# Seven buffers instead of four between two matrix layers, with a smaller GpSimd DMA scratch

## The chip, the core and the metric

The kernel runs on one core of one Trainium2 chip. The metric is the device time of one execution in microseconds (us), as the median of several runs; lower is better. TensorE (PE) multiplies, VectorE (DVE), ScalarE (ACT) and GpSimd (POOL) work on elements, and SyncE (SP) issues nearly all DMAs.

## The reference

Block-causal attention feeds one wide layer pair, which feeds a second one with a three-way maximum:

```python
scores = where(block_i >= block_j, q @ k.T / 8, -1e9)       # 4 batches, 8 heads, 576 tokens, dim 64
x = (softmax(scores) @ v).reshape(2304, 512)
h = maximum(x @ w_in, 0)                                    # 512 -> 2048
x = (s * (h * h) + b) @ w_out                               # 2048 -> 512
h = maximum(maximum(x @ w1, x @ w2), x @ w3)                # 512 -> 768
out = h @ w_out2                                            # 768 -> 512
```

## The kernel before, in words

**Precision.** TensorE reads a reduced 32-bit format, so each operand is kept as two halves, a high part and the remainder, and a product is three matmuls (high by high, high by low, low by high). Making the halves is a copy on ACT or DVE and a subtraction on DVE (`sub_to`, L364). The weights arrive as 64-bit floats; `convert` loads a tile of 128x512 (L679) and rebuilds 32-bit floats with a clamp (L683), a rescaling on ACT or POOL, and three bit operations (L691, L695, L700) on DVE.

**Stages.** First comes attention, 16 head pairs in turn; the result lies in `xf`, 128 partitions by 4 slabs by 2304 tokens, and `normalize` (L791) divides by the softmax sums, which come back through DRAM (`scr`, L785). Then comes the first layer pair, on five chunks of tokens (512, 512, 512, 384, 384). Its inner dimension of 2048 is 16 tiles `f_` of 128, and the kernel takes the first 8 (`HF = 8`) for all chunks and then the last 8. The second layer pair follows and isn't touched.

**The stretch that the change concerns.** While attention ends, not all weights are prepared. So for chunks 0 and 1 all of the first layer runs first: `l1(c, f_)` for `f_` 0 to 7 and both chunks, 16 tiles of 12 matmuls, each followed by four ACT steps and one subtraction on DVE, which leave a tile of 128x1024 (both halves) in a buffer of the strip `h1`. Only then the second layer `l2(c, f_, k)` runs, again 12 matmuls for each chunk and `f_`, adding into all eight PSUM banks. `h1` has four buffers (`HAT1`, four places of 1024 words in the big SBUF tile `arena`), so the tiles of `f_` 0 to 5 go out to DRAM (`hscr`, L952, "away"), and those of 6 and 7 stay. The second layer therefore starts with 6 and 7 (`late_`), and `l1_back` (L961) fetches the other twelve tiles, each into the buffer that a tile just used has left:

```python
late_ = [HF - 2, HF - 1] + list(range(HF - 2))
...
        if i + 2 < HF:
            for c in range(2):
                l1_back(c, late_[i + 2])
```

**Places in `arena`.** `places` lays out the strips one after another: 8 tiles of `w_in`, 4 of `x1`, 8 of `w_out`, then `h1`; `RN` is the end. The attention operands (`kq_at`) lie at the end of the same tile, counted back from `RN`. The split input of chunk 1 (`x1b`, written by `split_x(1, "x1b")`) borrows four of the `w_out` places.

**Order.** `Sched` records each operation with its reads and writes and, at the end, `run` makes one list by a plan: each engine takes, among the operations whose inputs are there by the plan's costs, the one that was recorded first (shifted by the table `off`). On the chip each engine works through its list in that order, SP its list of DMA issues too. A different number or place of buffers thus changes the order on every engine. The `stg` strip holds weight tiles while they are converted, and `prepare_direct` orders the tiles that are wanted first.

Of the kernel before, what the change touches and what calls it, by code (L numbers as in the profile page):

```python
# [20 lines left out]
KT = DM // 128  # L21
NF, NG = FF // 128, F2 // 128
# [3 lines left out]
NU = 4  # L26
NEG = -2.0 ** 100
NK = 5
EPS = 1e-9


# [17 lines left out]
def f32(ap):  # L49
    return ap.bitcast(F32)  # L50
# [15 lines left out]
def c_dve2(n):  # L66
    return n / 1.92 + 68
# [6 lines left out]
def c_acts(n):  # L74
    return n / 1.2 + 93
# [6 lines left out]
def c_pool(n, ptr=False):  # L82
    return 0.83 * n + (243 if ptr else 160)
# [187 lines left out]
def tile_attention_moe(ctx: ExitStack, tc: tile.TileContext, qk, vp, w_in, w_out, s_, b_, w123, w_out2, out):  # L271
    nc = tc.nc
# [6 lines left out]
    banks = Banks(ps)  # L279
# [5 lines left out]
    def places(at, n, *sizes):  # L285

        out_ = []
        for m, w in zip(n, sizes):
            out_.append([at + w * i for i in range(m)])
            at += m * w  # L290
        return out_ + [at]

    IAT, XAT1, OAT, HAT1, RN = places(0, (NF // 2, KT, NF // 2, 4), 1024, 1024, 1024, 1024)
    XAT, HAT, WAT_, VAT, HATB, rn = places(0, (14, 2, 8, NG, 2), 2 * HN, 2 * HN, 512, 1024, 2 * HN)
    assert rn <= RN
    kq_at = [RN - 4352 * i for i in (2, 1)]
    arena = Arena(p0.tile([128, RN], F32R, name="arena"))
# [33 lines left out]
    def words2(t):  # L333
# [1 line left out]
    rings = dict(raw=Strip(other, RAWAT, 2 * S), k0=Strip(other, K0AT, 256, lambda t: t[0:64]), nmx=Strip(other, NMAT, NB), den=Strip(other, DENAT, 36),  # L335
                 rdt=Strip(other, RDAT, 128), rawv=Strip(other, RVAT, 17 * D, lambda t: t.rearrange("p (a c) -> p a c", c=D)),
                 k1=Strip(arena, kq_at, 1152), q1=Strip(arena, [x + 1152 for x in kq_at], 1024, two), kq2=Strip(arena, [x + 2176 for x in kq_at], 2176),
                 x1=Strip(arena, XAT1, 1024, two), x1b=Strip(arena, OAT[2:6], 1024, two), h1=Strip(arena, HAT1, 1024, two),
                 x=Strip(arena, XAT, 2 * HN, two), v=Strip(arena, VAT, 1024, two), h=Strip(arena, HAT + HATB, 2 * HN, two), w=Strip(arena, WAT_, 512, two),
                 wb=Strip(other, WB2, 512, two), wv=Strip(other, WV2, 1024, two),  # L340
                 stg=Strip(other, SAT, 1024, words2), nrm=Strip(other, NAT, 512), rg1=Strip(other, RGAT1, 512), part=Strip(other, PAT + [UAT[0] + 512 * i for i in range(4)], 512), t1=Strip(other, TAT[0:2], HN), t2=Strip(other, TAT[2:4], HN), tt=Strip(other, TAT[4:], HN), y=Strip(other, WV2, 512),
# [6 lines left out]
    def mul_to(e, dst, src, m, ptr=False):  # L348

        if e == "ACT":  # L350
            nc.scalar.activation(out=dst, in_=src, func=AF.Copy, scale=m)  # L351
        elif e == "DVE":
            nc.vector.tensor_scalar(out=dst, in0=src, scalar1=m, scalar2=None, op0=ALU.mult)  # L353
        else:
            nc.gpsimd.tensor_scalar(out=dst, in0=src, scalar1=m, scalar2=1.0, op0=ALU.mult, op1=ALU.mult)  # L355
# [18 lines left out]
    def CFG_E(k, **c):  # L374
        return {e: c[e] for e in CFG["ew"][k]}
# [264 lines left out]
    def denominators(b, DEN):  # L640

        def f(e):
            nc.vector.tensor_scalar(out=DEN.ap, in0=DEN.ap, scalar1=EPS, scalar2=None, op0=ALU.add)
            nc.vector.reciprocal(DEN.ap, DEN.ap)
# [152 lines left out]
    def split_x(c, ring="x1"):  # L797
        c0, n = CHUNKS[c]
        for k in range(KT):
            X = rings[ring].get()  # L800
            xs1[c, k] = X
            src = xf[:, k, c0:c0 + n]

            def f(e, X=X, src=src):
                mul_to(e, X.ap[:, 0, 0:n], src, 1.0)
            i = op(CFG_E("xhi", Pool=c_pool(n), ACT=c_acts(n), DVE=c_dve2(n)), 0, f, reads=[(XF, ("x", c, k))], writes=[(X, 0)], kind="xs", lock=True)

            def f(e, X=X, src=src):
                sub_to(e, X.ap[:, 1, 0:n], src, f32(X.ap[:, 0, 0:n]))
            j = op(CFG_E("xlo", DVE=c_dve(n), Pool=c_pooltt(n)), 0, f, reads=[(XF, ("x", c, k)), (X, 0)], writes=[(X, 1)], kind="xs", lock=True)  # L810
            xdone1.setdefault((c, k), []).extend((i, j))
# [143 lines left out]
    def l1_back(c, f_):  # L955

        n = CHUNKS[c][1]
        hs[c, f_] = u = rings["h1"].get()

        def f(e):  # L960
            nc.sync.dma_start(out=f32(u.ap[:, :, 0:n]), in_=hscr[HF * c + f_].rearrange("p (a c) -> p a c", a=2)[:, :, 0:n])  # L961
        load(1024 * n, f, reads=[(HS, (c, f_))], writes=[(u, 0), (u, 1)], kind="hf")
# [115 lines left out]
    HF, HG = NF // 2, NG // 2  # L1078
# [9 lines left out]
    PASSES = [(0, c) for c in range(2, NC)] + [(1, c) for c in reversed(range(NC))]  # L1088
    GORD = list(reversed(range(GROUPS)))
    order1 = [k for f_ in range(HF) for k in [("in", f_)] + [("out", f_ - 1)] * (f_ > 0)] + [("out", HF - 1)]  # L1090
    late_ = [HF - 2, HF - 1] + list(range(HF - 2))
    direct = [("in", f_) for f_ in range(HF)] + [("out", f_) for f_ in late_]
    aside = [(x, f_ + HF) for x, f_ in order1]
    aside2 = [k for i in range(HG) for k in [(i, w) for w in range(3)] + [("wo", i), ("wo", i + HG)]]
# [70 lines left out]
    SETS = (0, 1, 2, 3), (4, 5, 6, 7)  # L1165

    def accumulators(where, n):
        a = {i: banks.get((where[i],)) for i in range(n)}
        a["n"] = 0
        return a  # L1170
# [13 lines left out]
    for f_ in range(HF):  # L1184
        while ("in", min(f_ + 2, HF - 1)) not in ready:
            prepare_direct("w")
        for c in range(2):
            l1(c, f_, banks.get(SETS[0]), f_ < HF - 2)
    accs[0, 0], accs[0, 1] = (accumulators(SETS[1 - c], KT) for c in range(2))
    split_x(2)  # L1190
    for i, f_ in enumerate(late_):
        while ("out", late_[min(i + 2, HF - 1)]) not in ready:
            prepare_direct("w")
        for c in range(2):
            for k in range(KT):
                l2(c, f_, k, accs[0, c], 0, i)
        if i + 2 < HF:
            for c in range(2):
                l1_back(c, late_[i + 2])

    steps = [(n_, f_ + HF * s) for n_, (s, c) in enumerate(PASSES) for f_ in range(HF)]
    for i, (n_, f_) in enumerate(steps):
        s_now, c = PASSES[n_]
# [19 lines left out]
    for n_, G in enumerate(GORD):  # L1223
# [3 lines left out]
        for i in range(HG):  # L1227
            best = {}
            for w in range(3):
# [9 lines left out]
                c = seven((i, w), P1, dst, between)  # L1239
# [135 lines left out]
```

## Time and profile before

| | us |
|---|---|
| median of 3 runs | 859.22 |
| lowest and highest of them | 857.95, 864.2 |
| profiled execution, first to last instruction | 861.7 |
| TensorE busy in it | 841.9 |
| VectorE, ScalarE, GpSimd busy in it | 616.2, 443.9, 93.7 |

The profiled execution is one run of its own; it lies inside the span of the three. TensorE's busy time counts a matmul from its start to its modelled end, so waits within a running train of matmuls show only where a gap is left.

### The profile page before, as it was taken

How to read it: one execution, taken by the hardware profiler on the slowest of the kernel's cores; microseconds unless marked ns; L12 is line 12 of the kernel's file. 1: busy time of each engine (PE TensorE's matmuls, PEld its weight loads, DVE VectorE, ACT ScalarE, POOL GpSimd, SP SyncE). 2: the span in 40 equal slices, each digit the busy share in tenths (PEclk: the TensorE clock that was granted, in tenths of full speed). 3: DMA queues.
4: the chain of work that ended last, by engine and by line, in shares of the span. 5: the costliest groups of instructions: out<-in, count | busy, mean ns of one | idle time of the engine just before them, and what ended most of it. 6: DMA issues, size and time to landing. Idle time of an engine off the chain costs nothing.

```text
span 861.7 us, 13772 instructions
## 1 busy us (share of the span) xinstructions
PE 841.9 (98%) x4802; PEld 739.3 (86%) x4802; DVE 616.2 (72%) x1181; ACT 443.9 (52%) x990; POOL 93.7 (11%) x98
## 2 busy tenths in 40 slices
PE   7999999999979999999999999999999999999997
PEld 6777777678858889999998888889999999999996
DVE  7788999999943799935999333556669567847662
ACT  5899999989603676746766434441014111330112
POOL 6222233002200112100113000000000000000000
PEclk9999999999999999999999999999999999999999
DMA  7556675659699687996876010147675576647742
GB/s 249 164 185 215 197 245 163 228 208 317 218 330 314 226 284 251 340 408 224 280 256 241 25 49 0 50 147 230 210 221 175 188 227 208 204 153 232 225 135 74
DMA packets 74037, 178.72 MB, mean 207 GB/s; under 512 B 8816, under 2 KB 13168, under 8 KB 73968
## 3 DMA queue, kind: packets, MB, share of 16 engines
q1 hardware_dynamic: 73248, 177.12, 61.4%
q8 instruction: 38, 0.62, 0.3%
q10 hardware_dynamic: 720, 0.72, 0.2%
q14 instruction: 31, 0.25, 0.1%
HBM read 133.96 MB, written 43.85 MB: 206 GB/s over the span
## 4 chain that ended last, share of the span: by engine, by line
PE 82%; DVE 7%; DMA 6%; ACT 3%; issue 2%; SPq 0%; ACTq 0%; DVEq 0%
PE ps L367 78%; PE ps L560 4%; DMA bscr<-other 3%; DMA arena<-hscr 2%; DVE other L495 2%; DVE arena L364 1%; ACT other L499 1%; DMA other<-qk 1%; DVE arena L353 1%; DVE arena L461 1%; DVE other L364 1%; DVE other L747 0%; ACT other L351 0%; DVE other L700 0%; DVE other L695 0%
## 5 line engine op out<-in xcount | busy, mean ns | idle before, releaser
L367 PE MATMUL ps<-arena 128*128 128x384 f32 (+6 forms) x3758 | 749.3, 357 | 9.5 <-DMA arena<-hscr 5.0
L367 PEld LDWEIGHTS ps<-arena 128*128 128x128 f32 (+1 forms) x3758 | 665.9, 190 | 87.4 <-ACT other L499 10.2
L873 DVE TENSOR_TENSOR other<-ps,other 128x384 f32<-128x384 f32 x189 | 101.0, 554 | 64.2 <-PE ps L367 62.4
L364 DVE TENSOR_TENSOR arena<-other,arena 128x384 fp32r<-128x384 f32 (+3 forms) x173 | 119.3, 698 | 19.5 <-ACT arena L351 14.5
L351 ACT ACTIVATE arena<-other 128x384 fp32r<-128x384 f32 (+3 forms) x111 | 62.7, 570 | 85.0 <-DVE other L1242 54.8
L923 ACT ACTIVATE other<-ps 128x512 f32<-128x512 f32 (+1 forms) x80 | 44.0, 551 | 101.5 <-PE ps L367 101.3
L359 ACT ACTIVATE other<-ps 128x512 f32<-128x512 f32 (+1 forms) x138 | 73.0, 570 | 42.4 <-PE ps L367 32.3
L353 DVE TENSOR_SCALAR arena<-other 128x384 fp32r<-128x384 f32 (+3 forms) x68 | 37.2, 548 | 73.5 <-ACT other L935 69.9
L355 POOL TENSOR_SCALAR other<-other 128x512 f32<-128x512 f32 (+1 forms) x50 | 50.1, 1005 | 331.2 <-DVE other L683 237.1
L499 ACT ACTIVATE other<-ps,other 128x576 f32<-128x576 f32 (+4 forms) x144 | 78.5, 564 | 10.5 <-DVE other L495 9.9
L495 DVE TENSOR_REDUCE other<-ps 128x1 f32<-128x576 f32 (+4 forms) x144 | 68.2, 512 | 12.8 <-PE ps L367 5.0
L885 ACT ACTIVATE other<-ps 128x384 f32<-128x384 f32 x27 | 13.2, 490 | 114.9 <-PE ps L367 91.8
L351 ACT ACTIVATE other<-other 128x256 fp32r<-128x256 f32 (+3 forms) x105 | 52.3, 510 | 38.7 <-DVE other L683 28.1
L560 PE MATMUL ps<-ident,other 128*128 128x128 f32 x400 | 59.3, 286 | 4.5 <-ACT other L499 4.4
L935 ACT ACTIVATE other<-other,cst 128x512 f32<-128x512 f32 (+1 forms) x80 | 61.8, 772 | 2.0
L367 PE MATMUL ps<-other 128*64 128x64 f32 (+5 forms) x640 | 55.0, 313 | 0.6 <-ACT other L351 0.6
L560 PEld LDWEIGHTS ps<-ident,other 128*128 128x128 f32 x400 | 46.5, 146 | 8.7 <-ACT other L499 6.8
L928 ACT ACTIVATE other<-other 128x512 f32<-128x512 f32 (+1 forms) x80 | 47.0, 587 | 1.7
L367 PEld LDWEIGHTS ps<-other 128*64 128x64 f32 (+1 forms) x640 | 29.7, 137 | 20.4 <-issue 15.6
L364 DVE TENSOR_TENSOR other<-other 128x256 fp32r<-128x256 f32 (+1 forms) x85 | 42.1, 508 | 3.4 <-ACT other L351 3.2
L695 DVE SCALAR_TENSOR_TENSOR other<-other 128x512 uint32<-128x512 uint32 x56 | 38.3, 686 | 5.1 <-POOL other L355 3.8
L355 POOL TENSOR_SCALAR arena<-other 128x1152 fp32r<-128x1152 f32 (+4 forms) x31 | 35.9, 1171 | 44.3 <-PE ps L367 31.0
(35 smaller groups left out, 337.6 us busy)
## 6 DMA issues: line engine op xcount, KB each, us to landing
arena<-bscr SPq DMA_DIRECT2D x189, 256.0 KB, 3.1
other<-qk SPq DMA_DIRECT2D x30, 576.0 KB, 3.8
bscr<-other SPq DMA_DIRECT2D x63, 256.0 KB, 2.8
other<-w_out SPq DMA_DIRECT2D x22, 512.0 KB, 3.7
wscr<-other SPq DMA_DIRECT2D x22, 512.0 KB, 3.0
arena<-wscr SPq DMA_DIRECT2D x22, 512.0 KB, 6.4
other<-w SPq DMA_DIRECT2D x18, 512.0 KB, 5.5
other<-vp SPq DMA_DIRECT2D x16, 544.0 KB, 4.9
```

Source lines behind the costliest of these rows:

```text
L351: nc.scalar.activation(out=dst, in_=src, func=AF.Copy, scale=m)
L353: nc.vector.tensor_scalar(out=dst, in0=src, scalar1=m, scalar2=None, op0=ALU.mult)
L355: nc.gpsimd.tensor_scalar(out=dst, in0=src, scalar1=m, scalar2=1.0, op0=ALU.mult, op1=ALU.mult)
L359: nc.scalar.activation(out=dst, in_=src, func=AF.Copy)
L364: eng[e].tensor_tensor(out=dst, in0=a, in1=b, op=ALU.subtract)
L367: nc.tensor.matmul(o, l, r, start=start, stop=stop)
L495: nc.vector.tensor_reduce(out=NM.ap[:, u:u + 1], in_=v, axis=AX.X if n <= 512 else AX.XY, op=ALU.max, negate=True)
L499: nc.scalar.activation(out=ev, in_=v, func=AF.Exp, bias=NM.ap[:, u:u + 1], scale=1.0, accum_out=DEN.ap[:, d:d + 1])
L560: nc.tensor.transpose(TB.ap[:, 128 * i:128 * i + 128], x, ident)
L873: nc.vector.tensor_tensor(out=out_.ap, in0=bank.ap[:, 0:HN], in1=u.ap, op=ALU.add)
L928: nc.scalar.activation(out=r, in_=r, func=AF.Square)
L935: nc.scalar.activation(out=r, in_=r, func=AF.Identity, scale=s_t, bias=b_t)
```

## The change

The core asks for a DMA scratch of 1024 bytes for GpSimd where it took the default, and `h1` gets seven buffers, `2 * HOLD + 1` with `HOLD = 3`. Of chunks 0 and 1 the tiles of `f_` 5, 6 and 7 stay on chip (`late_` starts with them) and those of 0 to 4 go to DRAM: ten stores and ten loads, not twelve and twelve. The first load goes into the seventh buffer and is recorded ahead of the second layer; after each `f_` of it the next two follow. `x1b` borrows the `w_out` places 1 to 4, not 2 to 5, since `w_out` 5 is wanted first now. `RN` grows from 24576 to 27648 words, and with it the attention operands move by 3072 words.

```diff
+HOLD = 3
-    IAT, XAT1, OAT, HAT1, RN = places(0, (NF // 2, KT, NF // 2, 4), 1024, 1024, 1024, 1024)
+    IAT, XAT1, OAT, HAT1, RN = places(0, (NF // 2, KT, NF // 2, 2 * HOLD + 1), 1024, 1024, 1024, 1024)
-                 x1=Strip(arena, XAT1, 1024, two), x1b=Strip(arena, OAT[2:6], 1024, two), h1=Strip(arena, HAT1, 1024, two),
+                 x1=Strip(arena, XAT1, 1024, two), x1b=Strip(arena, OAT[1:5], 1024, two), h1=Strip(arena, HAT1, 1024, two),
-    late_ = [HF - 2, HF - 1] + list(range(HF - 2))
+    late_ = list(range(HF - HOLD, HF)) + list(range(HF - HOLD))
+    backs = [(c, f_) for f_ in late_[HOLD:] for c in range(2)]
-            l1(c, f_, banks.get(SETS[0]), f_ < HF - 2)
+            l1(c, f_, banks.get(SETS[0]), f_ < HF - HOLD)
     accs[0, 0], accs[0, 1] = (accumulators(SETS[1 - c], KT) for c in range(2))
+    l1_back(*backs.pop(0))
     split_x(2)
-        if i + 2 < HF:
-            for c in range(2):
-                l1_back(c, late_[i + 2])
+        for _ in range(2):
+            if backs:
+                l1_back(*backs.pop(0))
-    nc = bacc.Bacc("TRN2", target_bir_lowering=False, num_devices=1)
+    nc = bacc.Bacc("TRN2", target_bir_lowering=False, num_devices=1, dynamic_dma_scratch_size=1024)
```

Lines behind the new constant have numbers higher by one in the changed kernel. The plan moves instructions on every engine from the last quarter of attention on. Three places follow, before and after apart.

SP, its DMA issues around the start of the second layer; before, the rows start behind the first load (L961, `arena<-hscr`), so that the second to the fifth stand here (`other<-w_in` and `w_out` load weights, `wscr` stores prepared ones, `other<-scr` loads softmax sums):

```order
L679 DMA other<-w_out 128x1024
L961 DMA arena<-hscr 128x1024
L785 DMA other<-scr 64x384 x2
L961 DMA arena<-hscr 128x1024
L679 DMA other<-w_in 128x1024
L721 DMA wscr<-other 128x1024
L679 DMA other<-w_in 128x1024
L785 DMA other<-scr 64x384 x2
L961 DMA arena<-hscr 128x1024
L721 DMA wscr<-other 128x1024
L961 DMA arena<-hscr 128x1024
```

The same place now, from the first load (L962) to the fourth:

```order
L962 DMA arena<-hscr 128x1024
L680 DMA other<-w_out 128x1024
L962 DMA arena<-hscr 128x1024
L786 DMA other<-scr 64x384 x2
L680 DMA other<-w_in 128x1024
L680 DMA other<-w_out 128x1024
L786 DMA other<-scr 64x384 x2
L962 DMA arena<-hscr 128x1024
L722 DMA wscr<-other 128x1024
L680 DMA other<-w_out 128x1024
L962 DMA arena<-hscr 128x1024
```

Between the first load and the fourth stood five weight loads, two `wscr` stores and two pairs of `scr` loads; now four, one and two stand there, and the second load stands behind one other DMA where it stood behind four.

TensorE, the end of attention (L560 is a transpose, `arena 128x288` the last score product, `arena 128x512` the first layer) before:

```order
L367 MATMUL ps<-other 64x64 x10
L367 MATMUL ps<-arena 128x288 x4
L560 MATMUL ps<-ident,other 128x128 x25
L367 MATMUL ps<-other 64x512 x2
L367 MATMUL ps<-other 64x384 x2
L367 MATMUL ps<-other 64x256 x2
L367 MATMUL ps<-other 64x128 x2
L367 MATMUL ps<-other 64x64 x10
L649 MATMUL ps<-ident,other 36x128
L367 MATMUL ps<-arena 128x512 x564
```

And now:

```order
L368 MATMUL ps<-arena 128x320 x2
L368 MATMUL ps<-other 64x256 x2
L368 MATMUL ps<-other 64x128 x2
L368 MATMUL ps<-other 64x64 x10
L561 MATMUL ps<-ident,other 128x128 x21
L368 MATMUL ps<-arena 128x512 x3
L561 MATMUL ps<-ident,other 128x128 x4
L368 MATMUL ps<-other 64x512 x2
L368 MATMUL ps<-other 64x384 x2
```

The last score product moved ahead of the products with the values, and three matmuls of the first layer moved in ahead of the last four transposes.

VectorE in the same stretch, from the normalizing of chunk 2 (L791) on (L495 is the maximum of the scores, `arena<-xf` the splitting of chunk 1, the rest prepares weights) before:

```order
L791 TENSOR_TENSOR xf<-xf,other 128x512
L495 TENSOR_REDUCE other<-ps 128x1
L791 TENSOR_TENSOR xf<-xf,other 128x512
L364 TENSOR_TENSOR arena<-xf,arena 128x512
L495 TENSOR_REDUCE other<-ps 128x1 x2
L353 TENSOR_SCALAR arena<-xf 128x512 x2
L364 TENSOR_TENSOR arena<-xf,arena 128x512 x2
L495 TENSOR_REDUCE other<-ps 128x1
L695 SCALAR_TENSOR_TENSOR other<-other 128x512
L495 TENSOR_REDUCE other<-ps 128x1
L700 SCALAR_TENSOR_TENSOR other<-other 128x512
```

And now:

```order
L792 TENSOR_TENSOR xf<-xf,other 128x512 x2
L692 TENSOR_SCALAR other<-other 128x512
L684 TENSOR_SCALAR other<-other 128x512
L496 TENSOR_REDUCE other<-ps 128x1
L696 SCALAR_TENSOR_TENSOR other<-other 128x512
L496 TENSOR_REDUCE other<-ps 128x1
L701 SCALAR_TENSOR_TENSOR other<-other 128x512
L692 TENSOR_SCALAR other<-other 128x512
L496 TENSOR_REDUCE other<-ps 128x1
L696 SCALAR_TENSOR_TENSOR other<-other 128x512
```

The splitting of chunk 1 left this stretch for an earlier one, where the places of `x1b` no longer lie under the attention operands. From the second L791 to the last maximum of attention there were 15 instructions that are no maximum, ten of L364, L695 and L700 and five of L353, L683 and L691; now there are 11, six and five. Farther on, the list of the first layer has `f_` 4 ahead of `f_` 3, and the load of the `w_in` tile of `f_` 3 stands on SP behind two `w_out` loads and four `scr` loads that it stood ahead of.

## Rows read from the trace of the kernel before

**Rows 1.** The page's head and part 1: busy time, share of span, instructions.

```profile
span 861.7 us, 13772 instructions
PE 841.9 (98%) x4802; PEld 739.3 (86%) x4802; DVE 616.2 (72%) x1181; ACT 443.9 (52%) x990; POOL 93.7 (11%) x98
```

**Rows 2.** TensorE's waits: who waited for whom, total us, times, longest.

```profile
PE ps L367 <- DMA arena<-hscr: 5.0, 2, 2.7
```

**Rows 3.** TensorE's timeline: start, us, instruction, count, [idle before, ended by].

```profile
174.00 3.47 PE L560 MATMUL ps<-ident,other 128*128 128x128 f32 x16 [1.20 <-ACT other L499]
...
180.44 57.38 PE L367 MATMUL ps<-arena 128*128 128x512 f32 x252
...
240.09 5.73 PE L367 MATMUL ps<-arena 128*128 128x512 f32 x24 [2.27 <-DMA arena<-hscr]
248.52 16.65 PE L367 MATMUL ps<-arena 128*128 128x512 f32 x65 [2.69 <-DMA arena<-hscr]
```

**Rows 4.** The chain that ended last, 224 to 252 us: start, us, what.

```profile
229.69 10.35 DMA arena<-hscr
...
240.60 7.87 DMA arena<-hscr
```

**Rows 5.** SP's timeline of DMA issues, same columns as rows 3.

```profile
226.97 0.33 SPq L961 DMA_DIRECT2D arena<-hscr  x1
...
229.69 0.60 SPq L961 DMA_DIRECT2D arena<-hscr  x1
...
237.98 2.53 SPq L785 DMA_DIRECT2D other<-scr  x2
240.60 0.54 SPq L961 DMA_DIRECT2D arena<-hscr  x1
```

**Rows 6.** Stretches: busy us of PE, PEld, DVE, ACT, POOL; clock, DMA share, GB/s.

```profile
222.00:226.00 4.00, 4.00 (x19) 3.31 (x18) 3.98 (x9) 4.00 (x8) 0.00 (x0) 1.00 0.04 11
236.00:238.00 2.00, 1.82 (x9) 1.17 (x7) 1.41 (x3) 0.00 (x0) 0.00 (x0) 1.00 1.06 417
238.00:240.00 2.00, 0.00 (x0) 0.00 (x0) 0.00 (x0) 0.00 (x0) 0.00 (x0) 1.00 1.05 267
...
249.36:252.77 3.41, 3.41 (x10) 2.63 (x9) 2.92 (x7) 0.67 (x1) 0.00 (x0) 0.50 1.03 414
174.26:177.68 3.42, 3.42 (x18) 3.09 (x18) 3.38 (x9) 2.80 (x7) 0.72 (x1) 0.50 0.18 56
160.00:170.00 10.00, 9.97 (x91) 7.02 (x89) 9.96 (x21) 9.68 (x29) 0.00 (x0) 1.00 0.59 194
...
180.00:224.00 44.00, 44.00 (x211) 36.49 (x206) 42.13 (x79) 41.23 (x71) 9.42 (x8) 1.00 0.76 267
300.00:320.00 20.00, 20.00 (x93) 17.00 (x92) 19.43 (x38) 15.04 (x27) 3.51 (x3) 1.00 0.86 290
```

**Rows 7.** DMA issues from 224 to 254 us: count, KB each, median us to landing.

```profile
arena<-hscr SPq DMA_DIRECT2D x8, 512.0 KB, 10.3
...
other<-scr SPq DMA_DIRECT2D x4, 96.0 KB, 7.2
```

**Rows 8.** VectorE's timeline, same columns as rows 3.

```profile
161.00 0.68 DVE L364 TENSOR_TENSOR arena<-xf,arena 128x512 fp32r<-128x512 f32 x1
...
162.27 0.75 DVE L353 TENSOR_SCALAR arena<-xf 128x512 fp32r<-128x512 f32 x2
...
199.95 0.69 DVE L364 TENSOR_TENSOR arena<-other,arena 128x512 fp32r<-128x512 f32 x1
```

**Rows 9.** The page's part 3, DMA queues: packets, MB, share of 16 engines.

```profile
q1 hardware_dynamic: 73248, 177.12, 61.4%
...
q10 hardware_dynamic: 720, 0.72, 0.2%
```

**Rows 10.** The page's part 6, DMA issues: count, KB each, median us to landing.

```profile
other<-w_out SPq DMA_DIRECT2D x22, 512.0 KB, 3.7
```

**Rows 11.** Waits from 254 to 270 us, columns of rows 2.

```profile
DVE other L353 <- DMA wscr<-other: 9.5, 1, 9.5
```

## The prediction

> **What bounds the kernel now.** The page's head comes first: TensorE is busy for 841.9 of 861.7 us [rows 1], so only what stops or slows TensorE counts. TensorE's waits, listed by who ended them, come next: the largest is for the tiles that come back from DRAM, 5.0 us in two waits [rows 2]. TensorE's timeline gives them as 2.27 us before 240.09 and 2.69 us before 248.52 [rows 3], 4.96 us. The chain of waits names what ended them: two loads of 10.35 and 7.87 us [rows 4]. The stretches then show a second loss: from 249.36 to 252.77, right behind the waits, the granted clock is 0.50, that is 1.2 GHz and not 2.4 [rows 6].
>
> **When a load is asked for and when it is wanted.** The first layer and the start of the second run without a gap from 180.44 for 252 matmuls in 57.38 us [rows 3], 2.73 us for each tile of 12. Those 252 are 21 tiles: 16 of the first layer and five of the second. So the second layer starts at 180.44 + 16 x 2.73 = 224.1. Before the change the second load may start when two tiles of the second layer are done (229.6; SP issues it at 229.69 [rows 5]), and is wanted as the sixth tile, at 237.8: 8.2 us. It took 10.35. The fourth could go at 235.1 but was issued at 240.60 [rows 5], since SP stood at a pair of loads of softmax sums ahead of it (2.53 us from 237.98 [rows 5]); it then took 7.87. Both misses follow from 8.2 us being shorter than a landing in this stretch, with a median of 10.3 [rows 7].
>
> **The two waits.** Now the second load goes into the buffer of the first tile used (226.9) and is wanted as the eighth tile (243.3); the fourth may go at 232.3 and is wanted at 248.7. Each has 16.4 us. Against 10.35 that leaves 6.0 us, and 8.5 against 7.87. The first load is released by the store of a first-layer tile and can land before 226, where the DMA queues moved 11 GB/s [rows 6]. What is late next would be the DMA queue itself: behind the first load and up to the fourth stand eight transfers of 512 KB and four of 96 KB [rows 7], 4480 KiB or 4.59 MB. At 417 GB/s, the better of two neighbouring stretches, they take 11.0 us, and at 267, the worse one [rows 6], 17.2; from 226.9 they are through by 238 to 244, and the fourth is wanted at 248.7. I take the waits as gone: **-4.96 us**, with one of them (2.69) left as the other bound.
>
> A page of the Trainium skill bears on this. The row shows 417 GB/s over 2 us, and 414 over 3.41 us [rows 6]. The Trainium skill ("DMA: Bandwidth & Descriptors", section "Specifications") puts the limit of HBM for one core at about 358 GB/s; by that, an estimate from its figure, the 4.59 MB would take 12.8 us. Here the rows go above that limit for short stretches, and either rate leaves the fourth load ahead of its time.
>
> **The clock behind them.** 3.41 us at half the clock hold work for 1.70 us [rows 6]. It fell behind two gaps in TensorE's work, and the same clock was 1.00 from 180 to 224 [rows 6], where there is none. Without gaps it stays: **-1.70 us**; if one wait is left, 0.
>
> **Fewer stores and loads, another buffer place.** Two stores and two loads of 512 KB go. They lie beside TensorE's work, as all but two loads did, so nothing but the above. The GpSimd scratch holds nothing that this kernel moves: the page's two queues that carry data are filled by hardware [rows 9], and GpSimd issues no DMA, so its price is nothing. The Trainium skill ("SBUF — State Buffer", section "SBUF size: 192, 224, or 256?") calls that scratch the ring space of the DMAs that GpSimd issues; by that, a kernel whose GpSimd issues DMAs would have less room for them; none such is in this trace.
>
> **The end of attention.** Here the new order counts. VectorE is busy for 9.96 of the 10 us from 160 to 170 and ScalarE for 9.68 [rows 6], and TensorE then waits 1.20 us for the last exponentials [rows 3], with half the clock from 174.26 to 177.68 [rows 6]. Splitting and conversion leave this stretch: four fewer instructions of the larger kind between the second L791 and the last maximum. One of them starts 0.60 us after the one before (from 161.00 the following maximum starts at 161.60, and from 162.27 two small ones take 0.67) [rows 8], so 4 x 0.6 = 2.4 us less on VectorE. Besides, three matmuls of the first layer now fill the place in front of the last transposes. The bounds are 0 (ScalarE, nearly as full, sets the end) and 1.20 + 1.71 = 2.91 us (wait and low clock both go). I take **-1.0 us**: VectorE's 2.4 can't be had in full beside a ScalarE with 0.32 us to spare in ten.
>
> **What the displaced work costs.** It goes to the first layer's stretch, where VectorE is busy 42.13 of 44 us [rows 6]. The tight place is the `w_in` tile of `f_` 3. The list now puts its last subtraction behind that of tile (1, 2), which began at 199.95 and took 0.69 [rows 8]; another 0.69 gives 201.3. With `f_` 4 taken first, it is wanted as the ninth tile, at 180.44 + 8 x 2.73 = 202.3. It is on time by 1.0 us, so I put nothing; the bound above is that its load takes 10.35 us like those of rows 4 and not 3.7 [rows 10]: 6.65 - 1.0 = 5.65, with 1.7 of clock 7.35.
>
> **The sum.** -4.96 - 1.70 - 1.0 = -7.66 us. The profiled execution gives only its span, 861.7, which lies 0.3% above the median of the runs and inside their range. 861.7 - 7.66 = 854.0, a ratio of 0.9911; on the median of 859.22 that is **851.5 us**.
>
> **The rivals.**
>
> *The whole gap at the end of attention goes too.* For it: the first layer's matmuls stand where TensorE waited. Against: ScalarE. 861.7 - 4.96 - 1.70 - 2.91 = 852.1, on the median 849.7 us. Chance 0.20.
>
> *The weight tile comes late.* The tile of `f_` 3 stands behind more loads on SP, and VectorE has next to nothing to spare, so a late load delays what is queued behind its clamp on VectorE, the splitting of the first layer's results too. Against: the 1.0 us, and that this stretch ran without one wait. Between nothing and 7.35 us I take 2, nearer to the row in which such loads land in 3.7: 853.5 us. Chance 0.15.
>
> *One of the two waits stays.* The DMA engines are full from 236 to 240 (1.06, 1.05 [rows 6]), and now ten loads are asked for earlier in the same stretch. 2.69 + 1.70 back: 851.5 + 4.4 = 855.9 us. Chance 0.12.
>
> *Slower: VectorE stands behind a store in a full stretch.* VectorE once waits 9.5 us for a store to `wscr` to leave its buffer [rows 11]; in SP's list such stores stand behind `hscr` loads that wait for TensorE. No wait of TensorE follows there [rows 2]. The new list places stores and loads anew; were such a wait to fall between 300 and 320 us, where VectorE has 0.57 us to spare [rows 6], 8.9 us would reach TensorE, and with 1.7 of clock 10.6: 862.1 us. It turns the change into a loss from a wait of 7.66 - 1.70 + 0.57 = 6.5 us on. Against: the first loads now all stand earlier, and the store that follows the last of them is freed when the second layer's ninth tile is done, 248.7, some 13 us earlier than now. Chance 0.05.
>
> *The change does nothing here*, since another DMA in the queue sets the same ends: 859.2 us, chance 0.03. That the buffers aren't there can't be: the strip has seven places.
>
> **How the numbers follow.** The forecast keeps 0.45. Its own range is 850.0 to 853.0, from the bounds at the end of attention. The range to hold the time 8 times in 10 reaches from below the first rival to above the third: 847.5 to 857.5. The three runs of before lie 0.7% apart, so about 1% is what a measurement of this kernel can tell from no change. That line is at 850.6: faster by more holds the first rival nearly whole and a third of the forecast's range, 0.33; slower than 867.8 only two mishaps at once, 0.03; within 1% the rest, 0.64.
>
> **What would show it.** In the profile of the changed kernel the wait of TensorE for `hscr` loads should be gone from its list of waits, and the clock should be 1.00 from the start of the first layer to the end of the second. The second load should be issued near 227 and the fourth before 236. The stretch from the first matmul of the first layer to the first of chunk 2 should be 6.7 us shorter. At the end of attention the first layer should start about 1 us earlier, with a shorter wait in front of the transposes; no wait should stand in front of tile (0, 3). Wrong would make it: a wait for weights in the first layer, a clock that falls without a gap, or new waits behind VectorE after 290 us that eat the gain.

## The result and the profile after

The changed kernel took 852.97 us (median of 4 runs, 852.23 to 853.45); the kernel before, on the same chip, 861.34 us (4 runs, 857.95 to 864.2). The ratio is 0.990, 95% interval 0.987 to 0.993. Two later comparisons on other runs gave 0.990 (0.987 to 0.993) and 0.992 (0.989 to 0.995). So the change saves about 8 us in 860. The forecast of 851.5 us, a ratio of 0.991, was right: the measured median lies 1.5 us above it and inside its own range of 850.0 to 853.0. On the medians of the three comparisons the saving is 8.4, 8.2 and 7.4 us; the sum was 7.66.

The page of the changed kernel, its head and part 1 (compare [rows 1]): TensorE is busy 6.4 us less with the same 4802 matmuls, and the span is 10.6 us shorter than that of the profiled execution of before. Most of the 6.4 us is half clock that is gone: up to 290 us there were 13.7 us of it and now are 3.4, a difference that holds 5.1 us of work. Of these, 1.7 us belong to the start, where both kernels do the same work.

```profile
span 851.1 us, 13711 instructions
...
PE 835.5 (98%) x4802; PEld 735.5 (86%) x4802; DVE 616.2 (72%) x1191; ACT 441.8 (52%) x984; POOL 81.9 (10%) x94
```

TensorE's waits in the changed kernel, as in [rows 2] (who waited for whom, us in total, times, longest). All eight rows stand here, so that the reader sees what is missing: no row names `hscr`.

```profile
PE ps L561 <- ACT other L500: 2.9, 5, 0.9
PE ps L368 <- ACT other L500: 1.4, 4, 0.4
PE ps L368 <- ACT other L352: 1.2, 1, 1.2
PE ps L368 <- DVE arena L1041: 1.2, 1, 1.2
PE ps L368 <- DVE arena L365: 1.0, 2, 0.8
PE ps L368 <- DVE arena L462: 0.8, 1, 0.8
PE ps L368 <- ACT other L360: 0.7, 1, 0.7
PE ps L561 <- ACT other L360: 0.3, 1, 0.3
```

TensorE's timeline of the changed kernel, answering to [rows 3]. The row at 164.14 is a landmark that both kernels have (twelve small products of one unit of attention). The last transposes wait 0.44 us where they waited 1.20; three matmuls of the first layer stand ahead of the rest at 173.59; and from 177.82 on the first layer, the second and the start of chunk 2 run as one row, which the end of the view cuts off.

```profile
164.14 1.99 PE L368 MATMUL ps<-other 64*64 64x64 f32 x12
...
171.32 2.51 PE L561 MATMUL ps<-ident,other 128*128 128x128 f32 x21 [0.44 <-ACT other L500]
173.59 0.94 PE L368 MATMUL ps<-arena 128*128 128x512 f32 x3
...
177.82 112.37 PE L368 MATMUL ps<-arena 128*128 128x512 f32 x492
```

The same landmark in the kernel before, and then two rows of ScalarE's timeline, the first result of chunk 2's first layer that ScalarE reads, before (L923) and after (L924):

```profile
164.89 1.99 PE L367 MATMUL ps<-other 64*64 64x64 f32 x12
```

```profile
277.67 0.60 ACT L923 ACTIVATE other<-ps 128x512 f32<-128x512 f32 x1 [0.45 <-PE ps L367]
```

```profile
267.79 0.60 ACT L924 ACTIVATE other<-ps 128x512 f32<-128x512 f32 x1 [1.18 <-PE ps L368]
```

With these two landmarks, the small products in attention and ScalarE's first read of chunk 2, the 10.6 us between the two profiled executions split into four parts:

| stretch | before | after | difference |
|---|---|---|---|
| start of the span to the landmark in attention | 164.89 | 164.14 | -0.75 |
| landmark to the first layer's row | 15.55 | 13.68 | -1.87 |
| first layer's row to ScalarE's first read of chunk 2 | 97.23 | 89.97 | -7.26 |
| from there to the end of the span | 584.03 | 583.31 | -0.72 |

Three matmuls moved from the third stretch into the second; at 2.73 us for 12 they are 0.68 us. So the end of attention gained 2.55 and the two layers 6.58.

SP's timeline of the changed kernel, answering to [rows 5]: the first load from `hscr` goes out at 216.72, during the first layer, and the second to the fourth at 224.26, 228.36 and 231.05.

```profile
216.72 0.33 SPq L962 DMA_DIRECT2D arena<-hscr  x1
...
224.26 0.32 SPq L962 DMA_DIRECT2D arena<-hscr  x1
...
228.36 0.74 SPq L962 DMA_DIRECT2D arena<-hscr  x1
...
231.05 0.32 SPq L962 DMA_DIRECT2D arena<-hscr  x1
```

Stretches of the changed kernel with the columns of [rows 6]. The DMA engines are as full from 236 to 250 us as they were in the rows of before (1.02 and 1.03, at 415 and 417 GB/s), but TensorE is busy through all of it, and from 177.8 to 290 the granted clock is 1.00, 2.4 GHz.

```profile
236.00:240.00 4.00, 4.00 (x20) 3.30 (x19) 3.64 (x7) 0.68 (x2) 0.00 (x0) 1.00 1.02 415
240.00:250.00 10.00, 10.00 (x46) 8.29 (x45) 2.53 (x6) 0.00 (x0) 0.00 (x0) 1.00 1.03 417
...
177.80:290.00 112.20, 112.16 (x495) 92.33 (x494) 93.96 (x180) 72.23 (x121) 11.09 (x11) 1.00 0.82 295
```

### The profile page after: what moved, and what is told of

It reads as the page before. It is cut to its first block, busy times and chain, and to the rows that moved or that the text cites. A ratio compares the mean times of both kernels' runs of the same rounds, so it can differ in the third digit from the quotient of the medians.

```text
span 851.1 us, 13711 instructions
## 1 busy us (share of the span) xinstructions
PE 835.5 (98%) x4802; PEld 735.5 (86%) x4802; DVE 616.2 (72%) x1191; ACT 441.8 (52%) x984; POOL 81.9 (10%) x94
## 4 chain that ended last, share of the span: by engine, by line
PE 81%; DVE 9%; ACT 4%; DMA 3%; issue 2%; POOL 0%; ACTq 0%; SPq 0%; DVEq 0%; POOLq 0%
PE ps L368 78%; PE ps L561 4%; DVE arena L365 2%; DVE other L496 2%; ACT other L500 2%; DMA bscr<-other 1%; DVE other L365 1%; DVE arena L462 1%; ACT other L360 1%; DMA other<-pscr 1%; DVE other L701 1%; DMA other<-qk 1%; DVE arena L354 1%; DVE other L696 0%; POOL other L356 0%
## 5 line engine op out<-in xcount | busy, mean ns | idle before, releaser
L368 PE MATMUL ps<-arena 128*128 128x384 f32 (+7 forms) x3758 | 746.1, 357 | 5.4 <-ACT other L500 1.4
L352 ACT ACTIVATE arena<-other 128x384 fp32r<-128x384 f32 (+3 forms) x107 | 59.9, 567 | 83.8 <-DVE other L1245 54.2
L924 ACT ACTIVATE other<-ps 128x512 f32<-128x512 f32 (+1 forms) x80 | 44.0, 551 | 98.3 <-PE ps L368 97.1
L354 DVE TENSOR_SCALAR arena<-other 128x512 fp32r<-128x512 f32 (+3 forms) x72 | 40.8, 569 | 70.9 <-ACT other L936 67.1
L360 ACT ACTIVATE other<-ps 128x512 f32<-128x512 f32 (+2 forms) x139 | 73.5, 571 | 29.6 <-PE ps L368 20.6
L500 ACT ACTIVATE other<-ps,other 128x576 f32<-128x576 f32 (+4 forms) x144 | 78.7, 563 | 11.2 <-DVE other L496 10.6
L356 POOL TENSOR_SCALAR other<-other 128x512 f32<-128x512 f32 (+1 forms) x46 | 38.6, 842 | 293.3 <-DVE other L684 162.0
L561 PE MATMUL ps<-ident,other 128*128 128x128 f32 x400 | 57.0, 280 | 3.3 <-ACT other L500 2.9
L696 DVE SCALAR_TENSOR_TENSOR other<-other 128x512 uint32<-128x512 uint32 x56 | 38.4, 686 | 4.1 <-POOL other L356 2.7
L701 DVE SCALAR_TENSOR_TENSOR other<-other 128x512 uint32<-128x512 uint32 x56 | 39.8, 711 | 0.2
```

What stands on the lines that cost most here:

```text
L360: nc.scalar.activation(out=dst, in_=src, func=AF.Copy)
L368: nc.tensor.matmul(o, l, r, start=start, stop=stop)
L500: nc.scalar.activation(out=ev, in_=v, func=AF.Exp, bias=NM.ap[:, u:u + 1], scale=1.0, accum_out=DEN.ap[:, d:d + 1])
L561: nc.tensor.transpose(TB.ap[:, 128 * i:128 * i + 128], x, ident)
L701: nc.vector.scalar_tensor_tensor(out=lo_w, in0=hi_w, scalar=0x80000000, in1=lo_w, op0=ALU.bitwise_and, op1=ALU.bitwise_or)
```

## The experiments

The theory has two parts. The lead is the time from the moment a load's buffer comes free to the moment its tile is wanted; 8.2 us of it were too short, and 16.4 end the waits and the half clock behind them. And room for `x1b` beside the attention operands, with the order that follows from it, shortens the end of attention by 1 to 2.5 us. The rivals: the scratch is worth something; the seven buffers' order of tiles, and not the room, shortens the end of attention; two stores and two loads fewer make the difference; SP, standing at loads of softmax sums, makes the waits, and not the lead. In every kernel with another number of buffers or another room the planner writes the lists of the engines anew, so small waits elsewhere shift too.

**The scratch alone.**

```diff
-    nc = bacc.Bacc("TRN2", target_bir_lowering=False, num_devices=1)
+    nc = bacc.Bacc("TRN2", target_bir_lowering=False, num_devices=1, dynamic_dma_scratch_size=1024)
```

> The kernel before with the smaller GpSimd scratch alone. Main theory: the scratch holds nothing that this kernel moves, so the ratio to the kernel before is 1.000 (0.996 to 1.004), and the two waits for loads from hscr (5.0 us together) and a half clock of about 3.4 us behind them stay. Rival: the scratch itself is worth something (its memory or its set-up at the start); then some of the 8.4 us is had here already, 0.990 to 0.996.

Measured: 860.97 us, ratio 0.9993 (0.997 to 1.002). The scratch by itself costs and gives nothing. Every kernel with the larger `arena` below has the smaller scratch too; whether seven buffers fit beside the default one, no run tried. The instructions of every engine stand in the order of the kernel before, so this profile is a second one of the same program but for the scratch. TensorE's timeline there:

```profile
165.01 1.99 PE L367 MATMUL ps<-other 64*64 64x64 f32 x12
...
174.12 1.97 PE L560 MATMUL ps<-ident,other 128*128 128x128 f32 x16 [1.20 <-ACT other L499]
...
178.96 57.41 PE L367 MATMUL ps<-arena 128*128 128x512 f32 x252
238.68 7.36 PE L367 MATMUL ps<-arena 128*128 128x512 f32 x24 [2.31 <-DMA arena<-hscr]
247.03 43.13 PE L367 MATMUL ps<-arena 128*128 128x512 f32 x189 [0.99 <-DMA arena<-hscr]
```

The wait of 1.20 us before the transposes is the same, but here the sixteen transposes behind it take 1.97 us and not the 3.47 of [rows 3]: the clock did not fall. So from the landmark to the first layer it took 13.95 us, where the profile of before has 15.55. The waits for `hscr` are 2.31 and 0.99 us, and the clock falls behind the first of them:

```profile
240.16:243.57 3.41, 3.41 (x9) 2.64 (x8) 0.02 (x1) 0.00 (x0) 0.00 (x0) 0.50 1.02 413
```

ScalarE's first read of chunk 2 comes here at

```profile
274.56 0.60 ACT L923 ACTIVATE other<-ps 128x512 f32<-128x512 f32 x1 [0.46 <-PE ps L367]
```

so from the landmark in attention to there it takes 109.55 us, where the profile of before has 112.78.

**The room alone:** the larger arena with four buffers, twelve loads and a lead of 8.2 us.

```diff
-    IAT, XAT1, OAT, HAT1, RN = places(0, (NF // 2, KT, NF // 2, 4), 1024, 1024, 1024, 1024)
+    IAT, XAT1, OAT, HAT1, RN = places(0, (NF // 2, KT, NF // 2, 7), 1024, 1024, 1024, 1024)
+    HAT1 = HAT1[:4]
```

(the smaller scratch with it)

> The kernel before with the larger arena but four buffers in use as before: the operands of attention lie 3072 words higher, so the copy of x for chunk 1 no longer shares their room; stores and loads are as before. Main theory: the gain at the end of attention comes from this room alone, so the first layer starts 2 to 2.7 us earlier (near 178, not 180.4) and the wait of 1.20 us and the half clock at 174 go, while the two waits for hscr (near 5 us) and the half clock behind them stay: ratio 0.997 (0.995 to 0.999). Rival: that gain comes from the new order of the first layer's tiles with seven buffers; then the first layer starts at 180.4 as before and the ratio is 1.000.

Measured: 858.97 us, ratio 0.995 (0.993 to 0.997). TensorE's timeline:

```profile
165.34 1.99 PE L368 MATMUL ps<-other 64*64 64x64 f32 x12
...
172.53 2.51 PE L561 MATMUL ps<-ident,other 128*128 128x128 f32 x21 [0.45 <-ACT other L500]
174.80 0.94 PE L368 MATMUL ps<-arena 128*128 128x512 f32 x3
...
179.03 57.04 PE L368 MATMUL ps<-arena 128*128 128x512 f32 x249
237.20 3.02 PE L368 MATMUL ps<-arena 128*128 128x512 f32 x12 [1.12 <-DMA arena<-hscr]
241.41 5.74 PE L368 MATMUL ps<-arena 128*128 128x512 f32 x24 [1.20 <-DMA arena<-hscr]
247.62 3.01 PE L368 MATMUL ps<-arena 128*128 128x512 f32 x12 [0.47 <-DMA arena<-hscr]
251.41 38.83 PE L368 MATMUL ps<-arena 128*128 128x512 f32 x170 [0.77 <-DMA arena<-hscr]
```

From the landmark to the first layer it takes 13.69 us with three matmuls more in it, as in the changed kernel (13.68). Against the old order at full clock (13.95) that is 0.26 + 0.68 = 0.94 us. So the room makes this gain, not the number of buffers. (The first layer does not start 2 us earlier in absolute time, as expected, because this execution reached the landmark 0.45 us later.) The waits for `hscr` stay: 3.6 us in four pieces of at most 1.2, and, unlike what was expected, no half clock between 25 and 854 us. The gain in the median, 2.0 us against the scratch alone, is larger than 0.94 us; the rest is taken up below.

**The buffers alone:** the changed kernel with the attention operands back where they overlap `x1b`.

```diff
-    kq_at = [RN - 4352 * i for i in (2, 1)]
+    kq_at = [RN - 4096 - 4352 * i for i in (2, 1)]
```

> The changed kernel with the operands of attention put back where they share room with the copy of x for chunk 1, as before the change; seven buffers and ten loads stay. Main theory: the loads' lead of 16.4 us in place of 8.2 is worth 6.7 us by itself: no wait for hscr, no half clock behind it, ratio 0.9925 (0.991 to 0.994), and the first layer starts within 0.7 us of 180.4. Rival: the end of attention gains through the new order of tiles, so this kernel is as fast as the changed one, 0.990.

Measured: 855.05 us, ratio 0.991 (0.989 to 0.994). No wait for `hscr`, one row from the first layer on, and the end of attention as in the kernel with the scratch alone (13.96 us from the landmark, the wait of 1.2 us, full clock):

```profile
165.23 1.99 PE L368 MATMUL ps<-other 64*64 64x64 f32 x12
...
174.35 1.97 PE L561 MATMUL ps<-ident,other 128*128 128x128 f32 x16 [1.22 <-ACT other L500]
...
179.19 111.13 PE L368 MATMUL ps<-arena 128*128 128x512 f32 x489
```

So the kernel is 0.9% faster without any gain at the end of attention, which is most of what the whole change brings.

**Five buffers:** twelve loads as before, a lead of four tiles, 10.9 us.

```diff
-HOLD = 3
+HOLD = 2
-... x1b=Strip(arena, OAT[1:5], 1024, two) ...
+... x1b=Strip(arena, OAT[2:6], 1024, two) ...
```

> Five buffers in place of seven: two tiles of each chunk stay on chip and twelve are loaded, as before the change, but the first load has a buffer of its own and each later one is asked for 10.9 us ahead (four tiles of 2.73 us), not 8.2 or 16.4. Main theory (lead against landing): the loads that landed in 10.35 and 7.87 us now come in time or nearly so; the waits for hscr are together under 1 us, the clock stays 1.00 from 180 to 290, ratio 0.991 to 0.994. Rival (too many transfers): with twelve loads the DMA queue is as full as before, landings get longer with the number asked for, and one or two waits of over 2 us with a half clock stay: 0.995 to 1.000.

Measured: 854.35 us, ratio 0.991 (0.988 to 0.995), with no wait for `hscr`. The rival falls: twelve loads come in time with 2.7 us more of lead. Here `x1b` and the attention operands still share two of the four places, and a wait of 2.19 us stands before the transposes, with half clock behind it:

```profile
173.37 3.97 PE L561 MATMUL ps<-ident,other 128*128 128x128 f32 x23 [2.19 <-ACT other L500]
```

```profile
174.68:178.09 3.41, 3.41 (x17) 2.69 (x16) 3.41 (x7) 3.05 (x8) 1.65 (x2) 0.50 0.23 79
```

**Seven buffers, ten loads, the old lead.** The loads use four of the seven buffers in turn, each one freed three tiles ahead of its load's use.

```diff
+    h1b=Strip(arena, HAT1[5:] + HAT1[:2], 1024, two)
-        hs[c, f_] = u = rings["h1"].get()
+        hs[c, f_] = u = rings["h1b"].get()
-    l1_back(*backs.pop(0))
-            if backs:
+            if i and backs:
```

> The changed kernel with its seven buffers, its ten loads and its room as they are, but each load is given a buffer that comes free only three tiles ahead of its use, so its lead is 8.2 us as before the change, not 16.4. Main theory (lead against landing): waits for hscr of 3 to 5 us together come back, the first layer still starts near 178; ratio 0.995 (0.993 to 0.998), as the kernel with four buffers and the larger arena. Rival (fewer transfers, more buffers): with ten loads the queue is emptier and they land in time, waits under 1 us, ratio 0.990 as the changed kernel.

Measured: 855.74 us, ratio 0.9925 (0.990 to 0.995). The waits come back, but smaller than expected, 1.5 us in two. TensorE's timeline, and the chain of waits for the longer one:

```profile
244.46 3.06 PE L368 MATMUL ps<-arena 128*128 128x512 f32 x12 [0.23 <-DMA arena<-hscr]
248.82 41.55 PE L368 MATMUL ps<-arena 128*128 128x512 f32 x182 [1.31 <-DMA arena<-hscr]
```

```profile
238.82 9.96 DMA arena<-hscr
```

A load issued at 238.82 lands after 9.96 us, 1.76 more than 8.2 us of lead, and 1.31 us of that reach TensorE. So seven buffers do not end the waits unless they lengthen the lead. But the number 3 to 5 was wrong, and the ratio came out below the expected 0.995 (0.993 to 0.998). What SP waited for from 214 to 256 us shows a difference to the other kernels with this lead: its `hscr` loads waited for TensorE to free their buffers, and hardly for other DMAs (0.3 us; in the four others, 3.4 to 4.8 us).

```profile
SPq L962 <- PE ps L368: 12.9, 9, 3.0
```

So this run shows the short lead by itself: 8.2 us are too few even where SP issues nearly every load as soon as its buffer is free, and that costs 1.5 us. Whether the ten loads or their later place in the stretch keep SP free was not taken apart.

**SP's part in the second wait.** The loads of chunk 4's softmax sums, four pairs, leave SP's list and are issued by ScalarE.

```diff
-                    nc.sync.dma_start(out=N.ap[64 * j:64 * j + 64, 0:n], ...)
+                    (nc.scalar if c == 4 else nc.sync).dma_start(out=N.ap[64 * j:64 * j + 64, 0:n], ...)
```

(and the planner's record of it goes to ScalarE for chunk 4)

> The kernel before with the loads of chunk 4's softmax sums issued by ScalarE, so that SyncE has none of them between the loads from hscr; buffers, lead and scratch as before. Main theory: the second wait (2.7 us in the profile of before, 1.0 in that with the smaller scratch) is SyncE standing at such a pair of loads, so the fourth hscr load is issued near 235 and not at 239 to 241 and its wait falls under 1.2 us; the first wait (2.3 us) stays within 1 us of that, since 8.2 us of lead are too short by themselves: ratio 0.998 (0.995 to 1.001). Rival (landing alone): the waits are set by how long the loads take on a full queue, 3.3 to 5 us stay however early the fourth is issued, 1.000.

Measured: 862.27 us, ratio 1.000 (0.998 to 1.002). The fourth load goes out at 237.10, which is 59.0 us after the first layer's row begins; before, it was 60.2 us (240.60 [rows 5] and 180.44 [rows 3]). The third moved the other way, to 235.63, 57.5 us after that start where it was 52.0. TensorE's timeline:

```profile
236.54 3.01 PE L367 MATMUL ps<-arena 128*128 128x512 f32 x12 [1.05 <-DMA arena<-hscr]
240.69 5.73 PE L367 MATMUL ps<-arena 128*128 128x512 f32 x24 [1.14 <-DMA arena<-hscr]
246.96 3.04 PE L367 MATMUL ps<-arena 128*128 128x512 f32 x12 [0.54 <-DMA arena<-hscr]
250.76 39.53 PE L367 MATMUL ps<-arena 128*128 128x512 f32 x173 [0.76 <-DMA arena<-hscr]
```

Two long waits became four short ones, 3.5 us in all, the same pattern as with the room alone: the fourth load is in time now, and the second, third, fifth and sixth are late. But the edit did not free SP. The longest wait of SP's `hscr` loads for another DMA, from 214 to 256 us:

```profile
SPq L961 <- DMA other<-scr: 2.9, 1, 2.9
```

The third load waited until 235.56 us for a softmax-sum load to land that ScalarE had issued at 228.66. The kernel before has the same kind of wait: from 232 to 247 us ten of SP's issues waited for a DMA to land, and each waited for the one issued eight before it. That held up the fourth load. In the chain of rows 4, between its two loads, stands

```profile
240.06 0.45 SPq L785
```

This is the second of two loads of softmax sums. SP issued it when the second `hscr` load, eight issues before, had landed at 240.04. The fourth load went out right behind it, 5.5 us after its buffer came free by the prediction's sum (235.1), and landed in 7.87 us. So SP's waiting for DMAs that have not landed has a part in the second wait, and this rival stands beside the short lead. What holds an issue back until the eighth before it has landed, the program's own semaphores or the queue, is not shown.

**Five buffers and the room,** twelve loads: the second half of the question whether the saved transfers count.

```diff
-HOLD = 3
+HOLD = 2
-..., (NF // 2, KT, NF // 2, 2 * HOLD + 1), 1024, 1024, 1024, 1024)
+..., (NF // 2, KT, NF // 2, 7), 1024, 1024, 1024, 1024)
+    HAT1 = HAT1[:5]
-... x1b=Strip(arena, OAT[1:5], 1024, two) ...
+... x1b=Strip(arena, OAT[2:6], 1024, two) ...
```

> Five buffers with twelve loads and a lead of 10.9 us, and the larger arena of the changed kernel, so that the copy of x for chunk 1 has room of its own. Main theory: lead and room are all that the change brings, the two stores and two loads that it saves are worth nothing, so this is as fast as the changed kernel, ratio 0.990 (0.988 to 0.992), with no wait for hscr and none of over 1 us at the end of attention. Rival: the saved transfers count; then it stays at 0.993 with a wait or two in the second layer.

> The kernel with five buffers, twelve loads and the larger arena once more, since its first runs left it between two readings (its profile had no wait for hscr and a span of 850.2 us, its median 856.9 us). If lead and room are all that the change brings: within 0.2% of the changed kernel in the next run. If the two saved stores and loads count, or a lead of 10.9 us is short in some executions: 0.3 to 0.4% slower than that, ratio 0.993 to the kernel before.

Measured: 856.85 us, ratio 0.993 (0.990 to 0.996), and in the second comparison 855.06 us, 0.992 (0.989 to 0.994). The first ratio is the rival's, the second lies at the edge of what the theory expected. The first profile has no wait for `hscr`, the second one of 0.31 us:

```profile
248.31 42.00 PE L369 MATMUL ps<-arena 128*128 128x512 f32 x184 [0.31 <-DMA arena<-hscr]
```

**The changed kernel again,** beside each of these on the same chip.

> The changed kernel once more, beside the others on the same chip: ratio 0.990 (0.988 to 0.992); its runs should lie within 0.3% of each other with a granted clock of 0.996 or 0.997 each, where runs of before had 0.989 to 0.996, since the waits behind which the clock falls are gone.

> The changed kernel a third time, as the other side of that comparison on one chip: ratio 0.990 (0.988 to 0.992) to the kernel before; no wait for hscr, and half clock at the start and the end alone.

Measured: 853.84 us (850.14 to 855.73), ratio 0.990 (0.987 to 0.993), and 854.68 us (853.0 to 857.2), 0.992 (0.989 to 0.995). In the first comparison it was 0.4% ahead of five buffers with room, in the second 0.04%, with intervals that overlap both times. So with leads of 10.9 us and more the two saved stores and loads are worth nothing that these runs can tell.

The expectation that its runs would lie within 0.3% of each other was wrong: they spread over 0.5 to 0.7%, with granted clocks of 0.992 to 0.998. In the profiles the difference lies at the start, where every kernel does the same work. The stretch from 5 to 30 us, with the columns of [rows 6], of the first profile of the changed kernel, of the second, and of the kernel before:

```profile
5.00:30.00 25.00, 20.59 (x148) 17.08 (x149) 19.65 (x31) 16.05 (x48) 10.06 (x14) 0.93 0.73 242
```

```profile
5.00:30.00 25.00, 20.33 (x110) 17.04 (x109) 17.60 (x27) 13.55 (x39) 8.90 (x13) 0.80 0.65 222
```

```profile
5.00:30.00 25.00, 21.59 (x133) 17.79 (x134) 19.21 (x30) 15.64 (x46) 9.82 (x14) 0.86 0.72 241
```

The mean clock there is 0.93, 0.80 and 0.86. The second profile has its last transposes' row at 174.70 where the first has it at 171.32, and from 180 to 850 us it shows no half clock and no wait for `hscr` either.

No version tried beat the changed kernel.

## Why the prediction was right, point by point

**The lead against the landing** was right, and the runs show it. With a lead of 8.2 us the `hscr` loads are late in each of the five profiles that have it (5.0, 3.3, 3.6, 1.5 and 3.5 us in all), whichever buffers, room or queue go with it. With 10.9 us two of three profiles have no such wait and the third has 0.31 us; with 16.4 us none of four has one. So in these profiles 10.9 us are just enough and 16.4 leave room.

Two readings behind it were not right. "Both misses follow from 8.2 us being shorter than a landing" holds for the second load, which went out as soon as its buffer was free and took 10.35 us. The fourth took 7.87 us, less than 8.2; it was late because SP, waiting for earlier DMAs and last for the second load, issued it 5.5 us late. The prediction saw that SP stood there, but not what it waited for. A longer lead covers both, the landing and the late issue: with 16.4 us TensorE waited for neither. And the median of 10.3 us [rows 7] is the landing of one load: of the eight the trace gives a landing for that one alone. Other profiles bear the size out: 9.96, 9.78 and 9.13 us for `hscr` loads in the same stretch (seven buffers with the old lead, the scratch alone, the room alone).

**The two waits, -4.96, and the clock, -1.70.** The forecast was 6.7 us (6.66) for the stretch from the first layer to chunk 2; it measured 6.58, with the three matmuls that moved counted. The second and fourth loads went out at 224.26 and 231.05, as the prediction had it (near 227, in a first layer that starts 2.6 us earlier, and before 236). The size holds for that profile of before: in the one with the scratch alone the two waits are 3.3 us. There the clock fell between the waits. The 24 matmuls at 238.68 took 7.36 us where they took 5.73 before [rows 3], and the wait behind them was 0.99 and not 2.69: the half clock ran in time in which TensorE would have waited. So the two terms do not always add, and waits and clock cost 5.0 us in that execution and 6.7 in the one that the prediction read.

**The full DMA queue** was weighed rightly. The DMA engines moved 415 to 417 GB/s from 236 to 250 us after the change too, for ten loads in the same stretch, and with 16.4 us of lead TensorE felt nothing of it. The Trainium skill ("DMA: Bandwidth & Descriptors", section "Specifications") puts the limit of HBM for one core at about 358 GB/s; these rows lie above it for 14 us, so the measured rate decides.

**The end of attention, -1.0,** is the term with the largest difference. Between the two profiled executions it measured 2.55 us, near the larger bound (2.91), the rival in which the whole gap goes, which had a chance of 0.20. But 15.55 - 13.95 = 1.60 of that is half clock behind the 1.20 us wait, which the profile of before has and the three others with the same order and wait don't. What the order brings at full clock is 0.94 us, nearly what was taken. The reason given was right in part: VectorE and ScalarE stay nearly full (9.84 and 9.68 of 10 us from 160 to 170, before 9.96 and 9.68 [rows 6]):

```profile
160.00:170.00 10.00, 9.44 (x63) 6.67 (x65) 9.84 (x22) 9.68 (x30) 1.24 (x1) 1.00 0.84 250
```

The prediction's terms do not separate the room for `x1b` from the number of buffers; the room alone and the buffers alone show that it is the room that lets the splitting leave this stretch.

**The displaced work, 0,** was right: no wait stands between 177.82 and 290 us, so the weight tile came in time, and the rivals of the late tile and of the wait that stays fall with it. **The scratch, 0,** was right by its own run. **Slower through VectorE behind a store** did not come: nothing of 1 us or more stands after 290. The largest wait there is 0.81 us:

```profile
330.69 67.05 PE L368 MATMUL ps<-arena 128*128 128x384 f32 x384 [0.81 <-DVE arena L365]
```

**What the sum left out.** Between 7.66 and the 10.6 us of the two profiled executions lie 2.9 us. About half is the end of attention (2.55 for 1.0), half the start (-0.75) and the stretch after chunk 2's start (-0.72). Neither of the last two is shown to be the change's: two further profiles of the changed kernel reach the landmark 2.6 and 2.2 us later than before's, with more half clock or longer waits at the start, and the last stretch differs by 3 us among the kernels tried.

**Where luck comes in.** The stretch that the change reaches, from the landmark in attention to ScalarE's first read of chunk 2, takes 112.78 us in the profile of before and 109.55 in that with the scratch alone, and 103.65, 103.31 and 103.41 in the three of the changed kernel. By which pair one takes, the change is worth 5.9 to 9.5 us there. The forecast was read from the slower of the two, which had half clock at 174 us and behind its second wait; that the medians differ by 7.4 to 8.4 us, so near to 7.66, is in part luck.

**What does not add up.** The buffers alone give 0.86%, the room alone 0.48%, a sum of 1.3%; together they give 0.8 to 1.0% in three comparisons. The intervals allow a sum of 1.0. One reading is that part is shared: with the room alone the two waits of over 2 us became four of at most 1.2, and its runs had granted clocks of 0.992 to 0.996 and none above 859.73 us, where those of the scratch alone went down to 0.988 and up to 867.44. That would be half clock saved, which the buffers also save by taking the waits away. The clocks of the runs fit, but there is no trace of such a run, so this stays argued, not shown.

## What to carry to other kernels

Where tiles are put out to DRAM and fetched back, write down for each fetch when its buffer comes free and when its tile is wanted, and compare that lead with the landing time in the same stretch under its own load, not with the median of the page. If the lead is the shorter, more buffers can end the waits: one more did here, while ten loads for twelve with the old lead, or softmax-sum loads issued by another engine, left waits of 1.5 and 3.5 us. Look also at what the issuing engine itself waits for: a load that lands late can hold back the issue of others, whose waits then look like theirs. Before a small term is sized from one profiled execution, take a second profile of the same program: half clock behind the same wait was there in one and not in the next, and it was worth more than the term.

## What was not expected of the hardware

The clock does not fall behind every wait, nor always behind the same one. Behind the 1.20 us before the transposes it fell in one of four profiles with that order; behind 2.19 us in the same place it fell; behind pieces of at most 1.31 us in the second layer it fell in none of three profiles. At the same load it stayed up behind 2.27 us in the profile of before and fell behind 2.31 us in that with the scratch alone; in the profile of before it fell behind the next wait, of 2.69 us. Each of the four half-clock rows between 25 and 290 us lasted 3.41 us.

The runs of one program spread by 1%, in part through this. Of the 22 runs of the kernel before in the first comparison of experiments, the fastest had 858.53 us and a granted clock of 0.996, the slowest 867.76 us and 0.989. A mean clock lower by 0.007 over 860 us is 6.0 us of work at full clock not done, some two thirds of the 9.2 us between them.
